# Linear attention on Trainium2: phi_q transposed into tiles of its own, with long rows in DRAM

## The chip, the cores and the metric

The kernel runs on one core of one Trainium2 chip. The metric is the time of one execution on the device in microseconds (us). Three executions of the kernel before are given, and one further execution was profiled.

## What is computed

Two identical layers work on x, 2048 tokens by 640 features, in float32. Each layer has a linear attention with 32 heads of 20 features and then a dense block, each behind a layer norm and each added to its input:

```python
q, k, v = split(layernorm(x) @ wqkv)              # 32 heads of 20
pq, pk = q @ w_phi, k @ w_phi                      # per head
phi_q = concat([softmax(pq), softmax(-pq)], -1)    # 40 per head, 1280 in all
phi_k = concat([softmax(pk), softmax(-pk)], -1)
kv, z = phi_k.T @ v, sum(phi_k)                    # per head, over all 2048 tokens
x = x + ((phi_q @ kv) / (phi_q @ z + 1e-6)) @ wo
x = x + mish(layernorm(x) @ w1 + b1) @ w2
```

Since kv and z need every token, phi_q can't be used before the last phi_k is summed. It is kept in DRAM in between.

## The kernel before, in words

**Precision.** A large float32 product is done as three TensorE products of halves: each operand is split into a rounded part (`h` in a name) and the rest (`l`). So names such as `xth`/`xtl` (the transposed input) and `r1h`/`r1l`, `r2h`/`r2l` (weights) come in pairs. ACT writes the rounded part and DVE (L286 for the input) or POOL subtracts to give the rest.

**Blocks.** The tokens are worked on in 8 blocks of 256, each of two tiles of 128 tokens. The 1280 features of phi lie in 11 groups: ten of 120 (three heads) and one of 80 (two heads).

**First stage, `attend_first`.** For each block, x is normalized and transposed on TensorE (in layer 0), or loaded already transposed from `n2_d`, which the dense block of layer 0 wrote (`spill_turned`, transposes L315, DMAs L317). Then for each of the two token tiles there are three projections on PE, L344: key, value and query. The weights of keys and queries have w_phi folded in at the start of layer 0 (L237). Keys and queries pass through `features`: ACT copies the PSUM result, DVE takes the maximum and minimum of each head (L368), the maximum is subtracted (L369, on DVE for keys and on POOL for queries), DVE subtracts from the minimum (L371), ACT takes the exponential, DVE sums (L377) and takes the reciprocal (L378), and POOL multiplies (L379). A key tile then enters the sums `kva`, `kvz` (`one` in the profile) in 11 pairs of matmul records per token tile, L416. A query tile is transposed in place in squares of 32 by 32 by one DVE instruction (L425), and four DMAs (L429) write it to `e_d[b]`, one row of 256 tokens per feature, in runs of 32 tokens (128 bytes). These steps are generators that are advanced in turns, so that the steps of one tile lie between the projections of the next.

**Between the stages.** `finish_kv` multiplies the sums with a mask (L537), transposes them on PE (L545) and copies them to `kvb` (L549). `rest` holds the last query's second half of the projection and its later steps; its pieces are put between these.

**Second stage, `attend_second`.** `load(b)` brings phi_q of a block back: two tiles of 128x1280 (L528) with five groups each and one small tile (L529). `average` multiplies each group with `kvb` (L573, with 64 tokens as the stationary columns), DVE divides, the result is transposed and goes through the output projection (L344). In the dense block L695 and L737 are the two products.

**Order.** Each engine carries out its own instructions in a fixed order. In the first stage and the dense block a scheduler chooses this order from modelled times; in `attend_second` the order on PE and SP is that of the code, and so it is for SP at the start of layer 0. All DMAs that matter here are issued from SP. They use eight semaphores in rotation, so that each DMA waits until the one eight places before it has landed.

**Buffers.** `big_tile()` (5 buffers of 128x1280, float32) serves key tiles, the loaded phi_q tiles and the dense block. `pair_tile()` (`ol`, 6 buffers) serves small tiles. Query tiles live in two further places (`r` in the profile).

The code that the change touches:

Of the kernel before, what the change touches and what calls it, by code (L numbers as in the profile page):

```python
# [8 lines left out]
F32 = mybir.dt.float32  # L9
# [7 lines left out]
P = 128  # L17
# [7 lines left out]
BT = 2  # L25
BLK = BT * P
NB = S // BLK
# [3 lines left out]
EW = 2 * D  # L31
GW = 3 * (DH + 1)
# [10 lines left out]
def kernel(  # L43
# [13 lines left out]
    nc = tc.nc  # L57
# [6 lines left out]
    dram = ctx.enter_context(tc.tile_pool(name="dram", bufs=1, space=DRAM))  # L64
# [7 lines left out]
    def big_tile():  # L72
        return work.tile([P, EW], F32, tag="big", name="big", bufs=5)

    def x_tile():
        return work.tile([P, BT, D], F32, tag="x", name="xt", bufs=2)

    def pair_tile(dtype=F32R):
        return work.tile([P, 2, BLK], dtype, tag="ol", name="ol", bufs=6)

    def row_block(t, b):
        return t[b * BLK:(b + 1) * BLK, :].rearrange("(p t) d -> p t d", t=BT)

# [10 lines left out]
    kvb = const.tile([120, GP, P], F32, name="kvb")  # L94
# [3 lines left out]

    wp_d = dram.tile([2, 2, KD, P, D], F32, name="wp_d")

    e_d = [dram.tile([EW, BLK], F32, name=f"e_d{b}") for b in range(NB)]

    n1_d = [dram.tile([D, BLK], F32, name=f"n1_d{b}") for b in range(NB)]
    n2_d = [dram.tile([D, BLK], F32, name=f"n2_d{b}") for b in range(NB)]
# [191 lines left out]
    def row_tile():  # L296
        return work.tile([P, D], F32, tag="xn", name="xn", bufs=4)
# [10 lines left out]
        for t in range(BT):  # L308
            act(dst[t], src[t], AF.Identity, bias=stats[:, b, 1, t:t + 1], scale=stats[:, b, 0, t:t + 1])

    def spill_turned(rows, dst):

        dst = dst.rearrange("(j f) (t q s) -> t q f j s", f=32, t=BT, s=32)
        for t in range(BT):
            nc.vector.transpose(rows[t], rows[t])  # L315
            for q in range(4):
                nc.sync.dma_start(dst[t, q], rows[t][32 * q:32 * q + 32].rearrange("f (j s) -> f j s", s=32))  # L317

    def load_turned(src, tiles):

# [61 lines left out]
    def fetch(x_src, b, xt=None):  # L382
        xt = x_tile() if xt is None else xt
        nc.sync.dma_start(xt, row_block(x_src, b))
        return xt

    def attend_first(layer, x_src, first):


        def fetch_normed(b):  # L390
            if layer:
                return load_turned(n2_d[b], [row_tile] * 3)
            xt = fetch(x_src, b)
            norm_scale(b, [norm_stats(t, xt) for t in range(BT)])
            return xt

        pending = []

        def advance():
            for g in pending[::-1]:  # L400
# [20 lines left out]
        def queries(xts, i, ps=None):  # L421
            e = query_tile(i)
            yield from features(project(xts, i % BT, q_ws, 0) if ps is None else ps, e, True)

            nc.vector.transpose(e, e)  # L425
            b, t = divmod(i, BT)
            dst = e_d[b].rearrange("(j f) (t q s) -> t q f j s", f=32, t=BT, s=32)
            for q in range(4):
                nc.sync.dma_start(dst[t, q], e[32 * q:32 * q + 32].rearrange("f (j s) -> f j s", s=32))  # L429
                if b == NB - 1:  # L430
                    yield

        def values(xts, i, v):
            vv = v.rearrange("p (h d) -> p h d", d=DH + 1)
# [12 lines left out]
        if first is None:  # L447
            with tc.manual_schedule(engines={mybir.EngineType.SP}):
# [3 lines left out]
                xt = fetch_normed(0)  # L452
# [11 lines left out]
        for b in range(NB):  # L464
# [9 lines left out]
            for n, (kind, t) in enumerate(order):  # L474
                t = int(t)
# [10 lines left out]
                if b + 1 < NB:  # L486
                    if n == 0:
                        xt = fetch_normed(b + 1)
                    elif n == 2:
                        nxt = xt if layer else normed(b + 1, xt)  # L490
                    elif n > 2:
                        nxt.step()
                g = {"k": lambda: keys(xts, i, vs[t]), "q": lambda: queries(xts, i),
                     "v": lambda: values(xts, i, vs[t])}[kind]()
# [25 lines left out]

    def load(b):

        ta, tb, tc_ = big_tile(), big_tile(), pair_tile(F32)
        for t, g0 in ((ta, 0), (tb, 5)):

            src = e_d[b][120 * g0:120 * (g0 + 4) + P]
            src = bass.AP(tensor=src.tensor, offset=src.offset, ap=[[BLK, P], [120 * BLK, 5], [1, BLK]])
            nc.sync.dma_start(t.rearrange("f (g s) -> f g s", s=BLK), src)  # L528
        nc.sync.dma_start(tc_[:80, 0], e_d[b][1200:])  # L529
        return [(ta, tb)[g // 5][:, (g % 5) * BLK:(g % 5 + 1) * BLK] for g in range(10)] + [tc_[:, 0]]  # L530

    def finish_kv(kva, kvz, mask):

        acc, acz = row_tile(), row_tile()
        for src, dst, p1, n, w in ((kva, acc, P, 4, 120), (kvz, acz, P, 1, 120), (kvz, acz, 42, 1, 80)):
            c = 120 if w == 80 else 0
            nc.vector.tensor_tensor(dst[:p1, c:c + n * w].rearrange("p (n w) -> p n w", n=n),  # L537
                                    src[:p1, c:c + n * w].rearrange("p (n w) -> p n w", n=n),
                                    mask[:p1, :w].unsqueeze(1).to_broadcast([p1, n, w]), op=ALU.mult)
        yield  # L540
        for src, q0, n in ((acc, 0, 4), (acz, 4, 2)):
            ps = one_tile().rearrange("p (n c) -> p n c", n=4)
            for q in range(n):
                p1, w = (P, 120) if q0 + q < 5 else (42, 80)
                nc.tensor.transpose(ps[:w, q, :p1], src[:p1, 120 * q:120 * q + w], ident[:p1, :p1])  # L545
            if n == 4:
                act(kvb[:, :4], ps[:120], AF.Copy)
            else:
                nc.vector.tensor_copy(kvb[:, 4], ps[:120, 0])  # L549
                nc.vector.tensor_copy(kvb[:80, 5, :42], ps[:80, 1, :42])  # L550
        yield

    def attend_second(x_src, x_dst, acc, fetches, makes, fetch_next, begin_next):
        kva, kvz, o_ws, loaded, rest = acc
        rows = {}
# [7 lines left out]
        def average(b, t):  # L563

            phs = loaded[b]
            po = mm_tile()
            for g in range(G):
                n = 120 if g < 10 else 80
                w = GW if g < 10 else 42
                c, j = divmod(g, 8)  # L570
                for q in range(2):
                    s0 = t * P + 64 * q
                    nc.tensor.matmul(  # L573
                        po[64 * q:64 * q + 64, c, GW * j:GW * j + w], phs[g][:n, s0:s0 + 64],
                        kvb[:n, g // 2, 64 * (g % 2):64 * (g % 2) + w], start=True, stop=True)
            o = row_tile()
            den = work.tile([P, H], F32, tag="r", name="den", bufs=2)
            pv = [po[:, c, :(DH + 1) * n].rearrange("p (h d) -> p h d", d=DH + 1)
                  for c, n in ((0, 24), (1, 8))]
            hh = (slice(0, 24), slice(24, H))  # L580
            for c in range(2):
                nc.vector.tensor_scalar_add(den[:, hh[c]], pv[c][:, :, DH], DEN_EPS)
            nc.vector.reciprocal(den, den)
            for c in range(2):
                n = hh[c].stop - hh[c].start
                ins = nc.vector.tensor_tensor(o.rearrange("p (h d) -> p h d", d=DH)[:, hh[c]], pv[c][:, :, :DH],
                                        den[:, hh[c]].unsqueeze(2).to_broadcast([P, n, DH]), op=ALU.mult)
                div[0] = ins.ins
            rows.setdefault(b, []).append(o)
            if t == BT - 1:  # L590
                del loaded[b]
# [19 lines left out]
        with tc.manual_schedule(engines={mybir.EngineType.PE, mybir.EngineType.SP}):  # L611
# [25 lines left out]
            for b in range(NB):  # L637
# [30 lines left out]
                xt = xs.pop(b)  # L668
# [12 lines left out]
    def dense(x_src, x_dst, w1s, w2s, first, last):  # L681
        blocks = {0: first}
# [57 lines left out]
        def end(b):  # L740
            xt, _, pys = blocks.pop(b)
            dst = row_block(x_dst, b)
            if last and b == NB - 1:
                for t in range(BT):
                    for c in range(2):
                        cs = slice(c * HC, (c + 1) * HC)
                        nc.vector.tensor_tensor(xt[:, t, cs], pys[t][:, c, :HC], xt[:, t, cs], op=ALU.add)  # L747
                        if t == BT - 1:
                            nc.sync.dma_start(dst[:, t, cs], xt[:, t, cs])
                    if t < BT - 1:  # L750
                        nc.sync.dma_start(dst[:, t], xt[:, t])
                return
            mvs = []
            for t in range(BT):
                nc.vector.tensor_tensor(xt[:, t, :].rearrange("p (c d) -> p c d", c=2), pys[t][:, :, :HC],
                                        xt[:, t, :].rearrange("p (c d) -> p c d", c=2), op=ALU.add)
                if not last:
                    mvs.append(norm_stats(t, xt))
            if not last:
                norm_scale(b, mvs)  # L760
            nc.sync.dma_start(dst, xt)
            if not last:
                xn = [row_tile() for _ in range(BT)]
                normalize(b, xn, [xt[:, t, :] for t in range(BT)])
                spill_turned(xn, n2_d[b])

        ahead = [None] * BT

# [10 lines left out]
        for i in range(len(steps) + SKEW):  # L779
            if i < len(steps):  # L780
                b, pr = steps[i]
# [19 lines left out]
            if i <= KD:  # L801
                with tc.issue_after(exps[0]):
                    w = next(last_w2)
# [5 lines left out]
            if i >= SKEW:  # L809
                b, pr = steps[i - SKEW]  # L810
# [5 lines left out]
    with tc.block(schedule_with_timeline_sim=True):  # L816
        src, first = x, None
        for layer in range(LAYERS):
            last = layer == LAYERS - 1
            dst = out if last else x2_d  # L820
# [39 lines left out]
            src = dst  # L860
# [38 lines left out]
```

## Time and profile before

| | |
|---|---|
| three runs | 1397.06, 1398.32 and 1398.65 us; median 1398.32 us |
| the profiled execution | 1396.09 us, of which the span in the profile is 1394.3 us |
| granted TensorE clock | 0.999 |
| PE, DVE, ACT, POOL busy | 1380.7, 1075.5, 583.3, 440.0 us |
| DMA | 350035 packets, 286866 of them under 512 bytes; 169.57 MB |
| first stage of attention | to about 268 us in layer 0; about 728 to 945 us in layer 1 |

In the profile PE is TensorE, DVE is VectorE, POOL is GpSimd, SP is the engine that issues the DMAs. L-numbers are lines of the kernel before, unless the text says that they belong to the changed one. "A <- B" after a wait means that A stood still until B was done. A group's line gives output and input shapes, the count, the busy time, the mean of one in ns, and the idle time before it with what ended it. PEld is the loading of the stationary operand, which overlaps PE's matmuls.

### The profile page before, as it was taken

What the parts mean: (1) busy time and instruction counts of PE and PEld (TensorE: products, weight loads), DVE (VectorE), ACT (ScalarE), POOL (GpSimd) and SP (SyncE); (2) the same over time, 40 slices, a digit from 0 to 9 for tenths busy, and PEclk for the clock granted to TensorE, in tenths of its full rate; (3) what the DMA queues carried; (4) which work ended last, traced back from release to release, by engine and by line L of the source; (5) the groups of instructions that cost most, each with busy time, mean ns of one, the idle gap of its engine ahead of it and who ended that gap; (6) DMA issues with size and microseconds to landing.
All of it is one profiled execution on the core that took longest, in us unless ns stands there. A gap on an engine that the chain in (4) does not pass through costs nothing. (4 is left out here: it accounts for less than half of the span.)

```text
span 1394.3 us, 28137 instructions
## 1 busy us (share of the span) xinstructions
PE 1380.7 (99%) x11528; PEld 1367.0 (98%) x11528; DVE 1075.5 (77%) x1820; ACT 583.3 (42%) x973; POOL 440.0 (32%) x334
## 2 busy tenths in 40 slices
PE   7999999999999999999999999999999999999998
PEld 7999999999999999999999999999999999999998
DVE  5797877796698877788769988888767876777775
ACT  4444433321355454545454333332235444444443
POOL 1353443343422221222234434343342211211112
PEclk9999999999999999999999999999999999999999
DMA  8533333689633432343474333357976212333200
GB/s 328 162 79 54 67 52 58 184 228 307 235 86 95 114 84 62 83 114 95 122 261 87 71 57 58 65 107 231 288 257 200 76 25 72 95 95 95 75 22 20
DMA packets 350035, 169.57 MB, mean 122 GB/s; under 512 B 286866, under 2 KB 323458, under 8 KB 349906
## 3 DMA queue, kind: packets, MB, share of 16 engines
q1 hardware_dynamic: 349906, 167.78, 44.2%
q8 instruction: 90, 1.47, 0.4%
q14 instruction: 39, 0.32, 0.1%
HBM read 104.82 MB, written 62.91 MB: 120 GB/s over the span
## 5 line engine op out<-in xcount | busy, mean ns | idle before, releaser
L737 PE MATMUL mm<-r2h,ol 128*128 128x320 f32 x1280 | 304.7, 309 | 0.0
L721 POOL TENSOR_TENSOR ol<-big,ol 128x512 fp32r<-128x512 f32 (+1 forms) x98 | 129.8, 1324 | 483.5 <-ACT ol L720 407.3
L695 PE MATMUL one<-xtl,r1h 128*128 128x256 f32 x960 | 268.2, 279 | 0.0
L695 PE MATMUL one<-xth,r1l 128*128 128x256 f32 x960 | 268.0, 279 | 0.0
L695 PE MATMUL one<-xth,r1h 128*128 128x256 f32 x960 | 265.9, 279 | 0.0
L737 PEld LDWEIGHTS mm<-r2h,ol 128*128 128x128 f32 x1280 | 219.1, 188 | 0.0
L737 PE MATMUL mm<-r2l,ol 128*128 128x320 f32 x640 | 197.3, 309 | 0.0
L344 PE MATMUL mm<-r1h,xth 128*128 128x320 f32 x600 | 187.3, 312 | 0.0
L344 PE MATMUL mm<-r1h,xtl 128*128 128x320 f32 x600 | 186.0, 310 | 0.7 <-DVE xtl L286 0.7
L344 PE MATMUL mm<-r1l,xth 128*128 128x320 f32 x600 | 186.0, 310 | 0.0
L695 PEld LDWEIGHTS one<-xtl,r1h 128*128 128x128 f32 x960 | 180.4, 188 | 0.0
L695 PEld LDWEIGHTS one<-xth,r1l 128*128 128x128 f32 x960 | 180.4, 188 | 0.0
L695 PEld LDWEIGHTS one<-xth,r1h 128*128 128x128 f32 x960 | 179.6, 188 | 0.0
L710 DVE TENSOR_SCALAR big<-big 128x512 f32<-128x512 f32 (+1 forms) x98 | 57.1, 583 | 109.9 <-ACT big L708 109.7
L379 POOL TENSOR_TENSOR r<-r,r 128x1280 f32<-128x1280 f32 x32 | 75.8, 2368 | 163.1 <-DVE r L378 157.3
L737 PEld LDWEIGHTS mm<-r2l,ol 128*128 128x128 f32 x640 | 120.2, 188 | 0.0
L712 ACT ACTIVATE big<-big,two 128x512 f32<-128x512 f32 (+1 forms) x98 | 70.1, 715 | 116.2 <-DVE big L711 116.1
L708 ACT ACTIVATE big<-one,b1s 128x256 f32<-128x256 f32 x192 | 80.8, 467 | 90.1 <-PE one L695 89.6
L720 ACT ACTIVATE ol<-big 128x512 fp32r<-128x512 f32 (+1 forms) x98 | 61.0, 622 | 136.0 <-DVE big L719 135.9
L344 PEld LDWEIGHTS mm<-r1h,xth 128*128 128x128 f32 x600 | 112.8, 188 | 1.3
L344 PEld LDWEIGHTS mm<-r1h,xtl 128*128 128x128 f32 x600 | 112.7, 188 | 1.3 <-DVE xtl L286 1.0
L344 PEld LDWEIGHTS mm<-r1l,xth 128*128 128x128 f32 x600 | 112.8, 188 | 0.1
(129 smaller groups left out, 3156.1 us busy)
## 6 DMA issues: line engine op xcount, KB each, us to landing
e_d<-r SPq DMA_DIRECT2D x128, 160.0 KB, 4.0
big<-e_d SPq DMA_DIRECT2D x32, 640.0 KB, 6.6
x_d<-xt SPq DMA_DIRECT2D x23, 640.0 KB, 3.9
xt<-x_d SPq DMA_DIRECT2D x22, 640.0 KB, 4.3
n_d<-xn SPq DMA_DIRECT2D x176, 80.0 KB, 2.1
xt<-in_x SPq DMA_DIRECT2D x16, 640.0 KB, 5.9
xn<-x_d SPq DMA_DIRECT2D x28, 320.0 KB, 4.2
v<-n_d SPq DMA_DIRECT2D x30, 256.0 KB, 3.3
```

The lines of the kernel that those rows point to most:

```text
L344: nc.tensor.matmul(ps[:, :HC], a[:, sl], r, start=(k == 0 and n == 0), stop=(k == KD - 1 and n == 2))
L379: nc.gpsimd.tensor_tensor(eg, eg, r.unsqueeze(2).to_broadcast([P, 2 * H, DH]), op=ALU.mult)
L695: nc.tensor.matmul(ph[:, j, :], l, r, start=(n == 0), stop=(n == 3 * KD - 1))
L708: exps[0] = nc.scalar.activation(part(ta, 0)[:, j - js.start], ph[:, j, :], AF.Exp, bias=b1s[:, 2 * pr + j:2 * pr + j + 1]).ins
L710: nc.vector.tensor_scalar_min(e, e, E_CAP)
L712: nc.scalar.activation(r, n, AF.Ln, bias=two)
L720: nc.scalar.activation(ah[:, js], n, AF.Copy)
L721: nc.gpsimd.tensor_tensor(al[:, js], n, ah[:, js].bitcast(F32), op=ALU.subtract)
L737: nc.tensor.matmul(pys[t][:, c, :HC], l[:, j, sl], r, start=(f == 0 and n == 0), stop=(f == KF - 1 and n == 2))
```

## The change

For blocks 0 to 6 of each layer, phi_q is no longer transposed in place. Three DVE transposes per token tile (two of 640 columns, one of 96) write into tiles that belong to the block (two `big` and one `ol`). Column groups are picked with a stride so that one partition holds, for the five groups of a tile, the same feature; the tokens of a group lie next to one another in runs of 64. After the second token tile, twelve DMAs (L464 of the changed kernel) write the block to `e_d` in rows of 1280 bytes, and to `f_d` for the last 96 features. `load` then brings each whole tile back in one DMA with 5120 bytes in a row per partition (L561). Block 7 keeps the old form of transpose, in DRAM tile `g_d`.

So that 64 tokens of a group lie together, the tokens of a block are dealt to partitions in another order: x is loaded in the first stage of layer 0 by four DMAs of 32 partitions each in place of one, and `n2_d` has its columns in that order for layer 1. The last group is taken with 96 rows in place of 80, the first 16 of which meet zeros in `kvb` that two memsets provide.

The number of instructions on PE, ACT and POOL is the same; DVE has 58 more and SP 80 more. The scheduler's order differs in places on PE, DVE and POOL: among others, POOL's multiply of a block's second key stands behind the subtract (L369) of the next query instead of ahead of it.

```diff
+    def row_parts(t, b):
+        return t[b * BLK:(b + 1) * BLK, :].rearrange("(h t s u) d -> u h s t d", h=2, t=BT, u=2)
...
-    e_d = [dram.tile([EW, BLK], F32, name=f"e_d{b}") for b in range(NB)]
+    e_d = [dram.tile([2, P, EW], F32, name=f"e_d{b}") for b in range(NB - 1)]
+    f_d = [dram.tile([96, BLK], F32, name=f"f_d{b}") for b in range(NB - 1)]
+    g_d = dram.tile([EW, BLK], F32, name="g_d")
...
-                nc.sync.dma_start(dst[t, q], rows[t][32 * q:32 * q + 32].rearrange("f (j s) -> f j s", s=32))
+                nc.sync.dma_start(dst[q % 2, 2 * t + q // 2] if first_stage else dst[t, q],
+                                  rows[t][32 * q:32 * q + 32].rearrange("f (j s) -> f j s", s=32))
...
+        def fetch_parts(b):
+            xt = x_tile()
+            for q in range(4):
+                nc.sync.dma_start(xt[32 * q:32 * q + 32], row_parts(x_src, b)[q // 2, q % 2])
+            return xt
...
-            xt = fetch(x_src, b)
+            xt = fetch_parts(b)
...
-            nc.vector.transpose(e, e)
             b, t = divmod(i, BT)
-            dst = e_d[b].rearrange("(j f) (t q s) -> t q f j s", f=32, t=BT, s=32)
-            for q in range(4):
-                nc.sync.dma_start(dst[t, q], e[32 * q:32 * q + 32].rearrange("f (j s) -> f j s", s=32))
-                if b == NB - 1:
+            if b == NB - 1:
+                nc.vector.transpose(e, e)
+                dst = g_d.rearrange("(j f) (q t s) -> t q f j s", f=32, t=BT, s=32)
+                for q in range(4):
+                    nc.sync.dma_start(dst[t, q], e[32 * q:32 * q + 32].rearrange("f (j s) -> f j s", s=32))
                     yield
+                return
+            if t == 0:
+                blocks[b] = [big_tile(), big_tile(), pair_tile(F32).rearrange("p j s -> p (j s)")[:, :192]]
+            for c, dst in enumerate(blocks[b]):
+                src = e[:, EW - 96:].rearrange("p (j f) -> p j f", f=32)
+                if c < 2:
+                    src = e[:, 600 * c:600 * c + 600]
+                    src = bass.AP(tensor=src.tensor, offset=src.offset, ap=[src.ap[0], [32, 4], [120, 5], [1, 32]])
+                    dst = dst.rearrange("p (m g t s) -> p t m g s", m=4, t=BT, s=32)[:, t]
+                else:
+                    dst = dst.rearrange("p (j t s) -> p t j s", t=BT, s=32)[:, t]
+                nc.vector.transpose(dst, src)
+            if t == BT - 1:
+                for q in range(4):
+                    qs = slice(32 * q, 32 * q + 32)
+                    for c, (src, dst, m) in enumerate(zip(blocks[b], (e_d[b][0], e_d[b][1], f_d[b]), (4, 4, 3))):
+                        nc.sync.dma_start(dst.rearrange("(m f) (q x) -> q f m x", m=m, q=4)[q],
+                                          src[qs].rearrange("f (m x) -> f m x", m=m))
+                del blocks[b]
...
     def load(b):
...
+        if b < NB - 1:
+            for c, t in enumerate((ta, tb)):
+                nc.sync.dma_start(t, e_d[b][c])
+            nc.sync.dma_start(tc_, f_d[b])
+            groups = [t.rearrange("f (q g s) -> f g q s", q=4, g=5) for t in (ta, tb)]
...
         acc, acz = row_tile(), row_tile()
+        nc.vector.memset(acz[:42, 120:136], 0.0)
...
-                p1, w = (P, 120) if q0 + q < 5 else (42, 80)
+                p1, w = (P, 120) if q0 + q < 5 else (42, 96)
...
-                n = 120 if g < 10 else 80
+                n = 120 if g < 10 else 96
...
-                        po[64 * q:64 * q + 64, c, GW * j:GW * j + w], phs[g][:n, s0:s0 + 64],
+                        po[64 * q:64 * q + 64, c, GW * j:GW * j + w], phs[g][:, 2 * t + q],
```

More of the change, by code (lines that the diff above doesn't have):

```diff
@@ L309, in normalize, with spill_turned @@
             act(dst[t], src[t], AF.Identity, bias=stats[:, b, 1, t:t + 1], scale=stats[:, b, 0, t:t + 1])
-    def spill_turned(rows, dst):
+    def spill_turned(rows, dst, first_stage=False):
         dst = dst.rearrange("(j f) (t q s) -> t q f j s", f=32, t=BT, s=32)
@@ L397, in attend_first @@
         pending = []
+        blocks = {}
         def advance():
@@ L521, in load @@
     def load(b):
[L523 to L530, printed above, removed]
+        ta, tb, tc_ = big_tile(), big_tile(), pair_tile(F32).rearrange("p j s -> p (j s)")[:96, :BLK]
+        if b < NB - 1:
[3 more added lines that the diff above has]
+            groups = [t.rearrange("f (q g s) -> f g q s", q=4, g=5) for t in (ta, tb)]
+        else:
+            for t, g0 in ((ta, 0), (tb, 5)):
+                src = g_d[120 * g0:120 * (g0 + 4) + P]
+                src = bass.AP(tensor=src.tensor, offset=src.offset, ap=[[BLK, P], [120 * BLK, 5], [1, BLK]])
+                nc.sync.dma_start(t.rearrange("f (g s) -> f g s", s=BLK), src)
+            nc.sync.dma_start(tc_, g_d[EW - 96:])
+            groups = [t.rearrange("f (g q s) -> f g q s", q=4, g=5) for t in (ta, tb)]
+        return [groups[g // 5][:120, g % 5] for g in range(10)] + [tc_.rearrange("f (q s) -> f q s", q=4)]
     def finish_kv(kva, kvz, mask):
         acc, acz = row_tile(), row_tile()
+        nc.vector.memset(acz[:42, 120:136], 0.0)
         for src, dst, p1, n, w in ((kva, acc, P, 4, 120), (kvz, acz, P, 1, 120), (kvz, acz, 42, 1, 80)):
-            c = 120 if w == 80 else 0
-            nc.vector.tensor_tensor(dst[:p1, c:c + n * w].rearrange("p (n w) -> p n w", n=n),
+            c, c1 = (120, 136) if w == 80 else (0, 0)
+            nc.vector.tensor_tensor(dst[:p1, c1:c1 + n * w].rearrange("p (n w) -> p n w", n=n),
                                     src[:p1, c:c + n * w].rearrange("p (n w) -> p n w", n=n),
@@ L549, in finish_kv @@
                 nc.vector.tensor_copy(kvb[:, 4], ps[:120, 0])
-                nc.vector.tensor_copy(kvb[:80, 5, :42], ps[:80, 1, :42])
+                nc.vector.tensor_copy(kvb[:96, 5, :42], ps[:96, 1, :42])
         yield
@@ L571, in average @@
                 for q in range(2):
-                    s0 = t * P + 64 * q
                     nc.tensor.matmul(
-                        po[64 * q:64 * q + 64, c, GW * j:GW * j + w], phs[g][:n, s0:s0 + 64],
+                        po[64 * q:64 * q + 64, c, GW * j:GW * j + w], phs[g][:, 2 * t + q],
                         kvb[:n, g // 2, 64 * (g % 2):64 * (g % 2) + w], start=True, stop=True)
@@ L764, in end @@
                 normalize(b, xn, [xt[:, t, :] for t in range(BT)])
-                spill_turned(xn, n2_d[b])
+                spill_turned(xn, n2_d[b], True)
         ahead = [None] * BT
```

## The prediction

> **What bounds the kernel now.** I began with the page: how busy each engine is, and which chain ended last.
>
> ```profile
> PE 1380.7 (99%) x11528; PEld 1367.0 (98%) x11528; DVE 1075.5 (77%) x1820; ACT 583.3 (42%) x973; POOL 440.0 (32%) x334
> ...
> PE 44%; DVE 0%; issue 0%; DVEq 0%
> ```
>
> PE is idle for 13.6 of 1394.3 us. So nothing that the change relieves elsewhere can give more than a part of 13.6 us, while any new late arrival at PE is paid in full, since PE never has room to catch up. Next the waits, PE's and those around the spills (us in total, times, longest):
>
> ```profile
> PE mm L237 <- DMA raw<-in_wqk_t: 7.1, 3, 4.1
> ...
> PE mm L573 <- PE mm L573: 0.9, 2, 0.4
> PE mm L344 <- DVE xtl L286: 0.7, 1, 0.7
> PE one L416 <- POOL big L379: 0.3, 1, 0.3
> ...
> ACT r L116 <- DMA e_d<-r: 37.5, 10, 4.6
> SPq L429 <- DVE r L425: 191.5, 24, 19.5
> ```
>
> PE waits for DMA at the start only (7.1 us before 10.4 us; the last 4.7 us are the tail). No PE instruction waits for phi_q's way to DRAM and back. ACT waits 37.5 us for the old spills, but is busy 42%. What is left for PE to win in mid-kernel is some 2.6 us: 0.43 and 0.41 at the two L573 starts, and 0.6 and about 1.0 around 768 and 772 us, at the start of layer 1. In the DMA issues the old spill and load stand as
>
> ```profile
> e_d<-r SPq DMA_DIRECT2D x128, 160.0 KB, 4.0
> big<-e_d SPq DMA_DIRECT2D x32, 640.0 KB, 6.6
> ```
>
> Last I read each engine's timeline (start, duration) where layer 0's first stage ends, from 257 to 272 us, for there the least time lies between the other engines and PE:
>
> ```profile
> 261.16 1.45 DVE L377 TENSOR_REDUCE r<-big 128x64 f32<-128x1280 f32 x1
> 262.64 0.55 DVE L378 RECIPROCAL r<-r 128x64 f32<-128x64 f32 x1
> 264.16 1.55 DVE L368 TENSOR_REDUCE m<-r 128x32 f32<-128x640 f32 x2 [0.97 <-ACT r L116]
> ...
> 263.36 2.37 POOL L379 TENSOR_TENSOR big<-big,r 128x1280 f32<-128x1280 f32 x1 [1.34 <-PE mm L344]
> 265.68 1.27 POOL L369 TENSOR_TENSOR r<-r,m 128x640 f32<-128x640 f32 x1
> ...
> 265.46 2.54 PE L416 MATMUL one<-big,v 128*64 128x120 f32 x44
> ```
>
> Token tile 15's key multiply (L379) is done at 265.73; its 22 of the 44 L416 matmuls begin at 266.6 (half of 2.54 us after 265.46). That is 0.9 us of slack.
>
> **Transposes.** Per token tile of blocks 0 to 6 one transpose becomes three. The rows are
>
> ```profile
> L425 DVE STREAM_TRANSPOSE r<-r 128x1280 f32<-128x1280 f32 x32 | 47.7, 1490 | 3.6 <-POOL r L379 3.4
> L315 DVE STREAM_TRANSPOSE xn<-xn 128x640 f32<-128x640 f32 x44 | 36.3, 834 | 2.0 <-ACT xn L116 1.9
> ```
>
> Two sizes give 1.025 ns per column and 178 ns fixed, so 834 + 834 + 276 (96 columns) = 1.94 us instead of 1.49: +0.45 us, 28 times, +12.7 us on DVE. Strides within a row are not in the trace; bounds are 0 extra and twice the duration (+1.9 us more). In a steady block (29.1 us between like L416 steps of layer 1) the windows show DVE 77% busy from 120 to 240 us and 85% from 820 to 937 us, so 4.4 us or more is free, against 0.9 us for two tiles: hidden. Without that cover it would be 0.9 us a block.
>
> **Order on POOL.** In the changed kernel's instruction order the multiply of each block's second key stands behind the next query's subtract (L369) on POOL, and its reciprocal behind that query's two L368 on DVE. In a steady block the multiply ran 203.68 to 206.05 and PE needed it at 212.82; now the first L368 ends at 205.5, the subtract at 206.8, the multiply at 209.2: 3.6 us left, nothing lost. At the layer's end PE needs it sooner. ACT's copy of query 14 ends at 264.13; the first L368 ends at 265.0, the subtract at 266.3, and the second L368 and the reciprocal also at 266.3; the multiply then runs to 268.65. PE needs it at 266.6: PE stands still 2.1 us. Behind it queue the last nine L344 of a query half, L545 and every L573. Layer 1 repeats the pattern: L368 from 941.09, multiply from 943.2 to 945.6, needed at 943.55, 2.1 us. Both ends: +4.2, from 0 (the next query's copy earlier than before, or kept slack) to +6. A further doubt is that L371 of that query and the multiply both become ready at 266.3. At 762.44 an L369 on DVE that has a mean of 0.98 us took 2.98, because a POOL multiply ran from 762.12 to 764.75; DVE ended 0.67 us after it. So if DVE starts first at 266.3, POOL may be held 0.8 us. I take POOL first: it waits for its own engine, and DVE only started 0.03 us after a subtract's end at 207.28. The Trainium skill, "SBUF — State Buffer", section "SBUF: two separate sides", says that the two engines share a port pair as an exclusive lock, held for a whole instruction; the 2.98 us agree. By that rule with DVE first the sum is 1.6 us higher.
>
> **Start.** Each DMA on SP waits for the eighth before it. x of block 0 now takes four of these eight slots, so the second phi_bd load and raw3, raw4 and the 40-row piece wait for the first phi_bd load and raw0 to raw2 (issued about 1.1 us later), and the first two v-weight loads, issued at 8.82 and about 9.4, wait for raw4 and the 40-row piece, which landed by about 11.1 and 11.7: +2.3 us. The third waits for the mask load (itself behind an x part): 12 to 14 instead of 10.25. The splits made from them reach PE with 1.4 to 2.4 us to spare. Also block 1's x may land before or after 13.3, where DVE waited 1.04 us for it. Net +1.5, from 0 to +3.5.
>
> **Blocks 0 and 1 of each layer.** DVE is saturated there. In layer 0 key multiplies ended 0.9 to 2 us before their L416 (81.25 against 83.21, 88.06 against 88.99, 96.06 against 97.69); transposes add 0.45 ahead of each: +0.5 (0 to +2). In layer 1 the changed order on PE pulls apart the two L416 at 767 and 768.8 and puts the last xtl matmul later, so most of those 1.6 us of waits go: -1.2 (-1.6 to +1.5).
>
> **Loads at the stage change.** The second tile of load(0) reuses key 14's buffer, free only at 266.6, and block 6's last spills queue behind it on SP; load(1) waits for those to land, about 271, and lands at 275 to 277.4 (a load took 4.6 to 6.6 us). PE needs block 1 at 274.5, with the 2.1 us above at 276.6: 0 (0 to +1.5 per layer).
>
> **Nothing** for the rest: longer runs in spills and loads (PE waits for neither; their cover is the 8 us and more between a spill and its reuse), 12 spills a block instead of 8 (SP waits 191.5 us for transposes as it is), two memsets and the last group's 96 rows instead of 80 (matmul time goes by columns: L573's two forms have 224 and 212 ns), the order of columns in n2_d, the tail.
>
> Sum: 4.2 + 1.5 + 0.5 - 1.2 = +5.0. The profiled run took 1396.09 (span 1394.3, 1.8 around it); the median of three is 2.23 higher, with a spread of 1.6. So 1401.1 for a like run, 1403.3 for a median.
>
> **Rivals.** *Hidden:* POOL gets the multiply in time or query 14's copy comes earlier, and the start hides in PE's slack. For it: PE-bound, everything touched lies off the path. Against: 0.9 us of slack against 2.9 us of delay. Only +1.5 - 1.2 + 0.5 or less remains: 1398 to 1400.
>
> *Faster:* the layer-1 start and both L573 starts lose their waits (2.5 us) because transfers land earlier and DVE's order is better, and x in parts feeds DVE 1 us sooner at the start: -3.5, 1394.8. It decides if the key multiplies at the ends keep their place in time, within 0.9 us. Against: no PE wait names e_d, and PE's matmul spacing (147 ns for 320 columns) is alike in stretches with 34% and 74% DMA. A page speaks for it: the Trainium skill, "DMA: Bandwidth & Descriptors", "Specifications", gives 512 B as the least transfer for line rate, and 286866 of 350035 packets here lie under it. By that rule the transfers get shorter, yet the waits above bound what PE can gain.
>
> *Much slower:* the strided transposes take twice as long. DVE would then take 4.8 us more a block: 24.7 + 4.8 = 29.5 against 29.1 us in layer 1, 27.3 in layer 0, and, being in order, come late with xtl and the multiplies. At about 0.5 to 1 us a block, 14 blocks, beside the sum, that gives 1410 to 1417. Nothing in the trace has such strides. Loads missing their time at both changes would give 1405 to 1407.
>
> **Numbers.** Forecast (1401 to 1407) 0.55, hidden 0.22, faster 0.07, much slower 0.16. The range 1397 to 1412 holds the first two and a third of the last, some 0.82. A measurement here can tell about 0.2%, 2.8 us: faster means under 1395.5 (0.07), same 1395.5 to 1401.1 (0.23: hidden and the low edge of the forecast), slower above (0.70).
>
> **What would show it.** PE waiting some 2 us for POOL at the second L416 (L432 after) just ahead of L545, in both layers; three transposes of 0.83, 0.83 and 0.28 us; DVE some 12 us busier; first PE work on v weights 1 to 2 us later; packets well down with no gain. Wrong if PE's idle time stays near 13.6 us, if that L416 waits for nothing, or if transposes take over 1.2 us.

## The result, and the profile after

The changed kernel takes 1410.5 us (median of four runs, 1409.3 to 1418.1) against 1398.2 us before: 12.3 us more, a ratio of 1.0101 with a 95% interval of 1.0065 to 1.0137. It is slower, as forecast, but by two and a half times the 5 us that the sum gave. A second set of four runs had a median of 1411.0 us.

The page of the profiled execution (span 1407.9 us; the run took 1410.0). L-numbers are now those of the changed kernel: L353 is the old L344, L432 the old L416, L615 the old L573, L388 the old L379, L378 and L380 the old L369 and L371, L377 the old L368, L386 and L387 the old L377 and L378, L294 the old L286, L258 the old L250, L245 the old L237. L459 is the new transpose and L561 the new load.

```profile
PE 1384.6 (98%) x11528; PEld 1369.2 (97%) x11528; DVE 1073.7 (76%) x1878; ACT 584.4 (42%) x973; POOL 444.7 (32%) x334
...
DMA packets 214612, 171.22 MB, mean 122 GB/s; under 512 B 150162, under 2 KB 183426, under 8 KB 214482
...
PE 92%; DVE 2%; DMA 2%; issue 1%; POOL 1%; SPq 0%; ACT 0%; DVEq 0%; POOLq 0%; ACTq 0%
...
e_d<-big SPq DMA_DIRECT2D x112, 160.0 KB, 2.6
big<-e_d SPq DMA_DIRECT2D x28, 640.0 KB, 7.0
```

The change does what it says: 135000 packets fewer, and a spill lands in 2.6 us, not 4.0. It brings PE nothing, since PE never waited for it (the run with the new form in blocks 2 to 5 alone, below, bears this out). PE's idle time has grown from 13.6 to 23.3 us, and PE is called busy for 3.9 us more, though it does the same matmuls. PE's waits (us in total, times, longest) name the places:

```profile
PE mm L245 <- DMA raw<-in_wqk_t: 9.9, 5, 4.3
PE one L432 <- POOL big L388: 4.8, 2, 2.8
PE mm L615 <- DMA big<-e_d: 1.5, 1, 1.5
PE mm L615 <- PE mm L615: 0.9, 2, 0.4
PE mm L353 <- ACT xth L124: 0.8, 1, 0.8
```

Since both kernels issue the same number of matmuls, the start of PE's n-th matmul can be compared between the two traces. The lag of the changed kernel, in us, at points of the time before (it adds up to 13.6 and not 12.3, since the traced execution of the kernel before was 2.1 us quicker than its median, that of the changed kernel 0.5 us):

| stretch | lag at its end | step | forecast |
|---|---|---|---|
| start, to 29 us | 4.8 | +4.8 | +1.5 (0 to 3.5) |
| blocks 0 and 1 of layer 0, to 105 us | 6.2 | +1.4 | +0.5 (0 to 2) |
| blocks 2 to 6, to 258 us | 6.2 | 0 | 0 |
| end of the first stage and second stage of layer 0, to 345 us | 10.1 | +3.9 | +2.1, and 0 to 1.5 for loads |
| dense block, to 720 us | 10.3 | +0.2 | 0 |
| start of layer 1, to 800 us | 9.1 | -1.2 | -1.2 |
| blocks 2 to 6 of layer 1, to 930 us | 9.1 | 0 | 0 |
| end of the first stage of layer 1, to 1000 us | 13.6 | +4.5 | +2.1, and 0 to 1.5 for loads |
| the rest | 13.6 | 0 | 0 |

The timeline where the first stage of layer 0 ends shows the forecast mechanism (start, duration):

```profile
270.55 1.53 DVE L377 TENSOR_REDUCE m<-r 128x32 f32<-128x640 f32 x2
272.00 0.55 DVE L387 RECIPROCAL r<-r 128x64 f32<-128x64 f32 x1
272.75 2.96 DVE L380 TENSOR_TENSOR r<-m,r 128x640 f32<-128x640 f32 x1 [0.20 <-POOL r L378]
...
271.44 1.27 POOL L378 TENSOR_TENSOR r<-r,m 128x640 f32<-128x640 f32 x1 [1.61 <-DVE m L377]
272.67 2.36 POOL L388 TENSOR_TENSOR big<-big,r 128x1280 f32<-128x1280 f32 x1
```

Key 15's multiply runs to 275.0, behind query 14's subtract, and PE's second half of L432 starts at 275.1, after 2.0 us of waiting. Layer 1's end has the same order: PE waits 2.8 us for POOL there. The transposes (DVE groups by form) are a little cheaper than forecast, and hidden:

```profile
L459 DVE STREAM_TRANSPOSE big<-r 128x640 f32<-128x640 f32 x56 | 43.6, 814 | 5.0 <-POOL r L388 5.0
L459 DVE STREAM_TRANSPOSE ol<-r 128x96 f32<-128x96 f32 x28 | 6.5, 233 | 0.0
```

### The profile page after: what moved, and what is told of

It is laid out like the page before. It is cut to its first block, busy times and chain, and to the rows that moved or that the text cites. A ratio compares the mean times of both kernels' runs of the same rounds, so it can differ in the third digit from the quotient of the medians.

```text
span 1407.9 us, 28221 instructions
## 1 busy us (share of the span) xinstructions
PE 1384.6 (98%) x11528; PEld 1369.2 (97%) x11528; DVE 1073.7 (76%) x1878; ACT 584.4 (42%) x973; POOL 444.7 (32%) x334
## 4 chain that ended last, share of the span: by engine, by line
PE 92%; DVE 2%; DMA 2%; issue 1%; POOL 1%; SPq 0%; ACT 0%; DVEq 0%; POOLq 0%; ACTq 0%
PE mm L353 25%; PE mm L779 24%; PE one L737 24%; PE one L353 12%; PE mm L615 3%; PE one L432 2%; PE one L288 2%; DMA xt<-in_x 1%; DMA big<-in_phi_bd 1%; DVE r L386 0%; DMA big<-e_d 0%; DVE m L377 0%; PE one L245 0%; DVE big L380 0%; PE mm L245 0%
## 5 line engine op out<-in xcount | busy, mean ns | idle before, releaser
L353 PE MATMUL mm<-r1h,xth 128*128 128x320 f32 x600 | 187.3, 312 | 1.0 <-ACT xth L124 0.8
L353 PE MATMUL mm<-r1l,xth 128*128 128x320 f32 x600 | 186.3, 311 | 0.0
L353 PE MATMUL mm<-r1h,xtl 128*128 128x320 f32 x600 | 185.7, 310 | 0.0
L388 POOL TENSOR_TENSOR r<-r,r 128x1280 f32<-128x1280 f32 x32 | 77.5, 2423 | 181.0 <-DVE r L387 168.3
L353 PEld LDWEIGHTS mm<-r1h,xth 128*128 128x128 f32 x600 | 112.7, 188 | 2.5 <-ACT xth L124 1.0
L353 PEld LDWEIGHTS mm<-r1l,xth 128*128 128x128 f32 x600 | 112.8, 188 | 0.4
L353 PEld LDWEIGHTS mm<-r1h,xtl 128*128 128x128 f32 x600 | 112.7, 188 | 0.4
```

The costliest lines, as they stand in the source:

```text
L353: nc.tensor.matmul(ps[:, :HC], a[:, sl], r, start=(k == 0 and n == 0), stop=(k == KD - 1 and n == 2))
L388: nc.gpsimd.tensor_tensor(eg, eg, r.unsqueeze(2).to_broadcast([P, 2 * H, DH]), op=ALU.mult)
```

## The experiments

Lags below are read in the same way as in the table, against the kernel before. The runs of the kernel before that were made beside them had medians of 1398.25 to 1398.47 us. Each lag comes from one trace. The edits move lines, so L439, L393, L568 and L622 of two of these kernels are the changed kernel's L432, L388, L561 and L615.

**The start: whole loads of x.**

```diff
-            for q in range(4):
-                nc.sync.dma_start(xt[32 * q:32 * q + 32], row_parts(x_src, b)[q // 2, q % 2])
+            nc.sync.dma_start(xt, row_block(x_src, b))
```

> The changed kernel, but the first stage's x of layer 0 is loaded as before: one DMA of 128 partitions with 5120 bytes each per block (the tokens of a block of layer 0 therefore stand in another order than the second stage assumes). Theory A (the start costs 4.8 us because of how x is loaded): PE's lag behind the kernel before at its 40th instruction falls from 4.8 us to under 0.5, and the time from 1410.5 to about 1405.7. Rival (the start is late for another reason, such as the buffers of phi_q): the lag stays near 4.8 and the time near 1410.

Measured: 1406.96 us, a ratio of 1.0057 (1.0042 to 1.0072). The lag after the start is 1.3 us instead of 4.8. Theory A holds, up to a remainder of about 1 us; the kernel with the new form in blocks 2 to 5 alone, whose start is before's code, has a lag of 1.3 us there too, so the remainder may be no more than the spread of single traces.

**The start: four DMAs of 128 partitions.**

```diff
+            for q in range(4):
+                t, c = q // 2, slice((q % 2) * HC, (q % 2 + 1) * HC)
+                nc.sync.dma_start(xt[:, t, c], row_block(x_src, b)[:, t, c])
```

> As the run before, but x in four DMAs of 128 partitions, 1280 bytes each. Theory S (four DMAs take four of the eight semaphores, so later loads are issued late): lag of 4 to 5 us at the start, as in the changed kernel. Theory T (DMAs onto 32 partitions are slow and hold up the others in flight): lag under 1.5 us.

Measured: lag 0.8 us after the start (1409.4 us in its one run, which lost more at the ends: 4.5 and 5.9 us). Four semaphores are taken here too, with shorter runs, and nothing is lost. They do delay an issue: the first DMA of block 1's x is issued at 8.47 us, against 6.06 with whole loads. But DVE starts on it no later (12.96 against 13.13 us):

```profile
12.96 1.34 DVE L258 BATCH_NORM_STATS2 bn<-xt 128x6 f32<-128x320 f32 x3 [0.68 <-DMA xt<-in_x]
```

**The start: four DMAs of 32 partitions, long runs.**

```diff
+            for q in range(4):
+                nc.sync.dma_start(xt[32 * q:32 * q + 32], row_block(x_src, b)[32 * q:32 * q + 32])
```

> As the run before, but x in four DMAs of 32 partitions, 5120 bytes in one run for each partition. Theory S: lag of 4 to 5 us. Theory T by the number of partitions: also 4 to 5 us, with 2560-byte packets of other loads as slow as in the changed kernel (159 ns against 112). Theory T by the length of the runs: under 1.5 us.

Measured: lag 4.5 us (1410.8 us in its one run). So neither the semaphores alone nor the length of the runs explains the loss. What this kernel and the changed one share is that each DMA writes 32 partitions only. With that goes a smaller number of packets in each DMA (32 here, 64 in the changed kernel, 128 in the whole and the wide loads); no run here separates the two. The windows of 3 to 9 and 9 to 15 us show the loss (the last two columns are the DMA engines' busy share and GB/s), first for whole loads, then for this kernel:

```profile
3.00:9.00 6.00, 3.25 (x12) 2.71 (x12) 0.73 (x2) 0.90 (x2) 0.00 (x0) 1.00 1.00 342
9.00:15.00 6.00, 4.59 (x20) 4.27 (x20) 4.15 (x14) 2.51 (x5) 1.09 (x3) 1.00 1.04 383
```

```profile
3.00:9.00 6.00, 3.04 (x11) 2.50 (x12) 0.00 (x0) 0.00 (x0) 0.00 (x0) 1.00 1.03 272
9.00:15.00 6.00, 2.48 (x10) 1.95 (x10) 3.12 (x10) 1.59 (x3) 1.09 (x3) 1.00 1.02 241
```

The engines are as busy, but move 241 GB/s instead of 383; a packet of 5120 bytes takes 355 ns on average in the first 20 us instead of 219. The loads of weights share that, if less than expected: their packets of 2560 bytes take 137 ns instead of 111, not 159.

**The start alone, in the kernel before.**

```diff
-            xt = fetch(x_src, b)
+            xt = x_tile()
+            for q in range(4):
+                nc.sync.dma_start(xt[32 * q:32 * q + 32], row_parts(x_src, b)[q // 2, q % 2])
```

> The kernel before with the four-part load of x in the first stage of layer 0 alone (tokens of a block in another order than the second stage assumes). Theory A: PE lags 4.8 us after the start and keeps it: 1403. Rival: the start is late only together with the other changes: 1398 to 1399.5.

Measured: 1402.0 us, 1.0031 (1.0018 to 1.0044): +3.7 us from this part alone, a little less than theory A's 4.8. The profiled run (1405.5 us) isn't typical: it lost 8.4 us at the start, of which about 4 while the granted clock was 0.5, from 21.6 to 31.8 us. It and the slowest one (1409.3 us) have a mean granted clock of 0.996, the other eight 0.999 or 1.000.

**The ends: key 15's multiply first.** DVE's two L377 of query 14 were ordered behind key 15's reciprocal, and POOL's subtract behind its multiply.

```diff
+        late = pool_sub and i == NT - 2
         for s, op in ((0, ALU.max), (1, ALU.min)):
-            nc.vector.tensor_reduce(m[:, s], eh[:, 1], axis=AX.X, op=op)
+            with tc.issue_after(ends["rec"]) if late else nullcontext():
+                nc.vector.tensor_reduce(m[:, s], eh[:, 1], axis=AX.X, op=op)
...
+        with tc.issue_after(ends["mul"]) if late else nullcontext():
```

> The changed kernel with one order restored at the end of each first stage: the reciprocal and the multiply of key tile 15 stand ahead of the maximum and the subtract of query tile 14, on DVE and POOL. Theory P (the waits for POOL are the cost and add up): the reciprocal ends at 271.2 and the multiply at 273.6 against a need at 272.9, so the stall falls from 2.4 to 0.8 us in layer 0 and likewise in layer 1, where the lower granted clock after the stall (0.52, 1.4 us) goes as well: 3 to 5 us less, 1406 to 1407. Theory L (behind the stall stands the load of block 1, which waits for the last spills of block 6): in layer 0 PE waits for that load instead and gains nothing; 0 to 2 us less in all, 1408.5 to 1410.5.

Measured: 1409.7 us (1406.0 to 1413.8), which is the changed kernel's time within the spread. PE's waits say where the gain went:

```profile
PE mm L622 <- DMA big<-e_d: 3.3, 2, 1.9
PE one L439 <- POOL big L393: 2.2, 2, 1.5
```

POOL's share fell from 4.8 to 2.2 us and the load's rose from 1.5 to 3.3 us. The chain of waits between 268 and 292 us of this kernel passes through the load:

```profile
271.92 1.32 PE one L439 x22
273.25 0.02 SPq L568
...
274.18 4.44 DMA e_d<-big
278.61 0.02 issue
278.63 5.84 DMA big<-e_d
284.47 0.04 issue
284.52 1.29 PE mm L622 x24
```

PE's L439 of key 14 frees a buffer, for which SP waits at 273.25 to issue the second tile of load(0); behind that stand block 6's last spills; load(1) needs their buffers, so it waits for them to land at 278.6 and itself lands at 284.5. This chain does not depend on key 15. Theory L holds by these waits; the time alone, with its spread, would not decide.

**The same with whole loads of x.** The edits for whole loads of x and for key 15 first, together.

> x of layer 0's first stage in one DMA per block (tokens of a block in another order than the second stage assumes) and key tile 15's multiply ahead of query 14's subtract, with block 6 still in the new form. Theory L (the load of block 1 waits for block 6's last spills and for the buffers they hold): PE waits 2 to 4 us for that load in the two layers together, and the time is 1404 to 1406.5. Theory P (POOL's order is the whole cost of the ends): 1399 to 1401.

Measured: 1406.2 us, 1.0055 (1.0041 to 1.0069), 0.8 us below whole loads alone, with intervals that overlap. PE waits 3.9 us for the two loads and 2.2 us for POOL; with whole loads alone it was 0.5 and 4.8 us. Theory L again.

**Block 6 in the old form.** Conditions `b < NB - 1` become `b < NB - 2`, with a second `g_d`. Block 6 then holds no `big` buffers, and the scheduler, left to itself, returns to before's order at the end.

> The changed kernel, but block 6 too is transposed in place and spilled and loaded in the old form, so that no phi_q tile of block 6 sits in the five big buffers; the scheduler then also puts key tile 15's multiply ahead of query 14's subtract. Theory P plus L: both ends lose their extra, 4.1 us in layer 0 and 4.6 in layer 1, so about 1402. If the order alone mattered and the load not, the time would be that of the run with the order restored.

Measured: 1406.7 us (1402.9 to 1409.2), 1.0066 (1.005 to 1.0083). Its profiled run, 1402.9 us, has a lag of 5.5 us before the first end, 6.9 after it, and 6.5 from 800 us to the finish: of the 8.4 us of both ends 1.4 are left, and no PE wait names POOL or a load of phi_q any more. The median is above the forecast 1402, because the other three runs took 1405 to 1409; they have no trace, so what they lost is open. It isn't the granted clock, whose mean was 1.000, 1.000 and 0.999 in them; the start, which this kernel keeps, is a candidate.

**All cures together.** Whole loads of x, block 6 old, key 15 first.

> Both cures together: x of layer 0's first stage in one DMA per block (tokens of a block in another order than the second stage assumes), block 6 in the old form, key 15's multiply first. If start and ends add up: 1410.5 - 4.8 - 8.7 = 1397.0, what is left being the +1.2 us of layer 0's first blocks and the -1.0 us of layer 1's. If something else is in the way: above 1400.

Measured: 1398.8 us, 1.0006 (0.9997 to 1.0015): no difference from before, with the new form still in blocks 0 to 5. Start and ends account for the loss. Against whole loads alone, 8.2 us less come from the two edits at the ends.

**The new form in blocks 2 to 5 alone.** Token order and storage of the other blocks as before.

```diff
+    e_d = {b: dram.tile([2, P, EW], F32, name=f"e_d{b}") for b in range(2, NB - 2)}
...
+            xt = fetch_parts(b) if b in e_d else fetch(x_src, b)
...
+            if b not in e_d:
```

> The new form of phi_q (own tiles, long runs, whole-tile loads, x in four parts) in blocks 2 to 5 alone; blocks 0, 1, 6 and 7 as before, with before's order of tokens. If the whole cost of the change sits at the edges (start 4.8 us, blocks 0 and 1 1.3 us, both ends 8.5 us) and the middle costs nothing, PE's lag stays within 0.5 us up to the end of layer 0, and the time is 1397 to 1399.5, no change. If the four-part load of x or the longer transposes cost something in the middle too, PE falls behind between 100 and 260 us, and the time is over 1400.

Measured: 1398.9 us, 1.0005 (0.9996 to 1.0014). The lag is 1.3 us after the start (whose code is before's) and 1.3 to 1.4 at every point to 720 us; one wait for POOL (1.2 us) at the start of layer 1 adds 0.9. So the forecast of no change held, its 0.5 us of lag not. The middle costs nothing, and gains nothing either: four blocks in eight with whole-tile loads and long runs, and no time won. No version that was tried beats the kernel before.

**The changed kernel again.**

> The changed kernel again, on this chip. 1409 to 1412, with the spread of its first runs (1409 to 1418). If the lower granted clock comes with PE's pauses, a profile shows it again after one of the three pauses (start, end of a first stage), not necessarily after the same one.

Measured: 1411.0 us (1410.4 to 1411.2), 1.0088 (1.0073 to 1.0103). The lower clock did come again, and after both ends: 0.5 from 275.2 us for 3.4 us and from 954.4 us for 6.8 us. A window there (the third number from the end is the granted clock):

```profile
276.00:279.00 3.00, 3.00 (x17) 2.77 (x14) 1.01 (x3) 0.50 (x1) 0.00 (x0) 0.57 0.77 194
```

Its lag grows by 4.3 us at the start, 1.4 in blocks 0 and 1, 3.8 at the first end and 5.8 at the second. PE waits the same 4.8 us for POOL, but not for load(1).

## Why the forecast was right in kind and wrong in size

Of the 8.6 us between the lag of 13.6 and the sum of 5.0, the start has 3.3, blocks 0 and 1 of layer 0 have 0.9, the two ends 4.2 (8.4 against 4.2 for POOL and 0 for loads) and the dense block 0.2. In the 8.4, PE's waits for POOL are 4.8, that for the load is 1.5 and the half clock about 1.4; 0.7 isn't traced to a row. So two steps failed: at the start, the landing times that were taken from before; at the ends, that the loads were put at 0 and a lower granted clock was not considered. That 1410.5 us lies in the range of 1397 to 1412 is luck: its upper part was there for strided transposes of twice the time, and they cost nothing.

- **The start: the largest single term that failed.** It was put at +1.5 us and measured +4.8, +3.7 when done alone. The prediction reasoned from semaphores: which load waits for which. That count was right in its order, but took before's landing times for the loads waited for. Those became later: with DMAs of 32 partitions the transfers in flight move 234 GB/s from 9 to 15 us, not 380, and the eight slots pass the delay on (block 1's x is issued from 9.88 us, not at 5.82). Block 1's x, which the prediction put near 13.3 us, was waited for by DVE until 18.14. First the row of before, then that of the changed kernel:

```profile
13.32 1.67 DVE L250 BATCH_NORM_STATS2 bn<-xt 128x6 f32<-128x320 f32 x4 [1.04 <-DMA xt<-in_x]
```

```profile
18.14 1.67 DVE L258 BATCH_NORM_STATS2 bn<-xt 128x6 f32<-128x320 f32 x4 [3.27 <-DMA xt<-in_x]
```

- **Blocks 0 and 1 of layer 0.** Put at +0.5 (0 to 2), measured +1.4. DVE's L380 of a key took 2.33 us at 92.22, beside POOL's multiply from 91.50 to 93.87; ACT's exponential and the copy to xth queued behind it, and PE waited 0.8 us for xth. The trace of before already had such rows (2.98 us), so the term should have been costed by them, not by the added 0.45 us alone.
- **POOL's order at the ends.** 2.1 us each were forecast, and PE waited 4.8 us in all, the longest wait 2.8. The place, the cause and nearly the size were right, and POOL did go first, so that DVE's L380 took 2.96 us. But POOL's order was only one of two bounds: with it restored, PE waited for the loads instead. One edit, block 6 in the old form, removed both waits; it changes block 6's buffers, transposes, spills and loads, and with them the order that the scheduler chose. That the buffers are the cause is shown for the load, by the chain above; for POOL's order it is not shown.
- **Loads at the stage change.** Put at 0 (0 to 1.5 per layer), measured 1.5 us in layer 0 of the profiled run, with the chain that the prediction described (load(0) behind key 14, block 6's last spills behind that, load(1) behind their landing). What failed was its time: load(1) landed at 285.2, 279.0 without the lag of 6.2 us, against 275 to 277.4. The spills landed at 278.0 (271.8 without the lag, forecast 271), and then the load took 6.8 us instead of the assumed 4.6 to 6.6. In the second profile PE does not wait for the load; 3.4 us at half clock stand there, and the end costs 3.8 us all the same.
- **A term that was missing: the granted clock.** Part of PE's 3.9 us of extra busy time is matmuls at half clock after a stall. At layer 1's end the timeline has:

```profile
955.64 1.80 PE L432 MATMUL one<-big,v 128*64 128x120 f32 x22 [2.77 <-POOL big L388]
957.37 0.63 PE L353 MATMUL one<-r2h,xth 128*128 128x320 f32 x1
957.80 0.47 PE L353 MATMUL one<-r2l,xth 128*128 128x320 f32 x1
958.07 0.47 PE L353 MATMUL one<-r2h,xtl 128*128 128x320 f32 x1
```

The starts of these L353 lie 0.27 us apart instead of 0.147. The trace's record of the granted clock has 0.5 from 956.4 to 959.9 us, and the lag grows by about 1.4 us there. The window:

```profile
957.00:960.00 3.00, 3.00 (x14) 2.78 (x12) 0.90 (x3) 0.57 (x1) 0.00 (x0) 0.52 0.57 197
```

- **Start of layer 1.** Forecast -1.2, measured -1.2 (-0.9 in the second profile). The two waits that the prediction named are gone from PE's list, so the mechanism held. The exact size is luck: the trace of before has 0.35 and 0.73 us of idle time there, 1.1 together, where the prediction read 1.6. PE's idle time in mid-kernel, with the two of 0.43 us, was 1.9 us and not 2.6.
- **Hidden work.** The transposes (1.86 us a token tile against 1.94 forecast), the spills, the memsets and the 96 rows cost nothing, as forecast: the lag does not move between 105 and 258 us, nor between 800 and 930. DVE's busy time did not rise by 12 us, but fell by 1.8: the transposes took 8.4 us more, and other steps less, the xtl subtractions of 512 columns from xn above all (10.8 us against 16.6); those are among the steps that POOL held up before (2.84 us at 766.49).
- **The rivals.** That shorter transfers would help PE fell: the packets are shorter in sum, and the middle gains nothing. Twice the time for strided transposes fell too: 814 ns against 834 for the plain ones. "Hidden" fell because PE had 0.9 us to spare at the ends, and none at the start, where it already waited for loads. "Much slower" came near the time (1410 to 1417), but by a mechanism that wasn't at work. Nearer to the cause was the remark beside it, that loads missing their time at both changes would give 1405 to 1407.

## What to carry to other kernels

When one engine is 99% busy, look for a change's cost at the program's edges: the first loads, and the point where one stage's buffers must be empty for the next; in the steady middle everything that was added here was free. If a late step is found on one engine, ask what is late next before adding up the gain: here a load stood right behind POOL, and only an edit that removed both waits paid. Splitting a load by partitions is not the same as splitting it by columns (lags of 4.5 and 0.8 us), and a start that is bound by transfers must be costed by what each transfer moves per us.

## What the runs showed of the hardware

- With x in DMAs of 32 partitions each (six traces), the DMA engines were as busy (share 0.96 to 1.07) at 234 to 287 GB/s as with DMAs of 128 partitions (the other six, 0.97 to 1.04) at 311 to 383 GB/s, in the windows of 3 to 9 and 9 to 15 us. It was so with runs of 2560 and of 5120 bytes; the four DMAs of 128 partitions with 1280-byte runs had 323 and 311 GB/s.
- The granted clock fell to 0.5 in pieces of 3.4 us or two or three times that, at or soon after a pause of PE, but not after each: none in the middle of the profiled runs of the kernel before, of block 6 in the old form, of all cures together and of the middle blocks alone; one piece in the changed kernel (956 us), with whole loads (272), key 15 first (285) and both of these (962); two pieces with four wide DMAs (953) and with four long ones (275 and 958); three in the changed kernel's second profile (275 and 954) and in the kernel before with x in parts (22). By half of 3.4 us, a piece costs PE up to 1.7 us, an estimate. The pauses of PE near them were of 1.9 to 2.8 us at the ends, and of 1.0 and 0.9 us at the start of the kernel before with x in parts. The Trainium skill, "TensorE: Matmul & The Clock Gate", section "Part 1: The HAM clock gate", says that the clock halves after an idle window of about 3.4 us, and that the window runs freely, so that one kernel differs from run to run; the pieces of 3.4 us agree, but here less than 3.4 us of pause was enough. The lower clock does not explain the wide spread of the changed kernel's first runs (1409 to 1418): the mean granted clock was 0.998 in the slowest one as in the profiled one of 1410.0 us, and 0.997 in that of 1411.0. What the slowest lost stays open.
- A DVE step of 640 columns with two operands in SBUF that began while a POOL multiply of 1280 columns was running ended 0.68 us after it, however early it began: 2.96 us from 272.75 against POOL's end at 275.03. It was 0.68 or 0.69 us in all such pairs of every trace, 8 to 12 in each. This is what the Trainium skill, "SBUF — State Buffer", section "SBUF: two separate sides", describes as an exclusive lock.
